# Two chunks of a GEGLU kernel turned later, and two of its weight columns moved to seven-product blocks

## The chip, the cores and the metric

One Trainium2 chip, one core of it. The metric is the device time of one execution in microseconds (us), as the median of three runs. A profile is one further execution, recorded by the hardware profiler; its span runs from its first to its last instruction. Engines are named as in the profile: PE is TensorE (matmuls; PEld its weight loads), DVE is VectorE, ACT is ScalarE, POOL is GpSimd, SP is SyncE, which issues most DMAs. Each engine works through its own queue in order.

## The reference

```python
def reference(x, dft_seq_re, dft_seq_im, dft_hid_re, dft_hid_im, w_gate, w_up, w_down):
    xn = layernorm(x)                          # x: 1 x 2048 x 448
    a = xn @ dft_hid_re.T                      # 448 x 448
    b = xn @ dft_hid_im.T
    s = dft_seq_re @ a - dft_seq_im @ b        # 2048 x 2048
    h = gelu(xn @ w_gate) * (xn @ w_up)        # 448 x 1792 each
    g = silu(h @ w_down)                       # 1792 x 448
    return x + s * g
```

## The kernel before

Tokens lie on 128 partitions in 16 tiles of 128, four tiles to a chunk; so there are four chunks (c = 0 to 3) of 512 tokens. The 1792 columns of the gate and the up matrix are cut into 14 columns f of 128. fp32 operands are split into a high part (rounded to the multiplication format, copied by ACT) and a low part (the rest, subtracted by DVE); a product of two split operands is three matmuls (high x high, high x low, low x high). The feature axis of 448 is four blocks of 128, the last with copies in it.

**Entry.** Rows of x are loaded into `xr`, normalised there (`stats`: bn_stats and bn_aggr on DVE, root on ACT, `newton` and `norm` on DVE), transposed by PE against an identity (`turn_mm`, L167, four small matmuls into one PSUM bank) and split into `xth` and `xtl` (`turn_split`, L172 on ACT, L178 on DVE). After a chunk's last tile `whole` copies the high parts to a DRAM tile `xw` with an SP DMA (L189), and adds the low parts to it with an accumulating DMA that POOL issues (L190). Pieces of that fp32 copy are read back later into temporaries (`t_load`, L674) and turned into sums.

**Direct columns.** Columns 0 and 1 of all four chunks are multiplied directly: `gateup` or `gu_mm` (L325) makes gate and up of one column and one chunk with 22 matmuls of 512 columns; `act` (L351 to L356) makes the gelu, the product and the split result `hs`. `down_one` (L376) makes one tile of the output of two columns: six matmuls of 448 columns into a PSUM bank, which is then copied (L385, ACT, the first pair of columns) or added (L387, DVE) into the sums `gacc`. The sums of chunks 0 and 1 stay in SBUF; those of chunks 2 and 3 are written to DRAM (`gsp`) after the first pair and read back in the second run.

**Two runs of blocks.** For columns 2 to 13, first for chunks 0 and 1 (run p = 0), then for chunks 2 and 3 (p = 1), `strassen` makes gate and up of one column for two chunks out of seven products with sums of the operands. A block has 41 matmuls of 512 columns where the operand sums `q` of the third and fourth feature blocks do not exist yet, and 39 where they do (L398, L410). Its results stand in PSUM banks 0 to 4: x1 in bank 0 (one product, read by ACT, L430, then a second product on top, read by the gelu, L456), x2 in bank 1, x3 and without `q` also x5 in bank 2, x4 in bank 3 (two products one after the other), x6 in bank 4. So x1 of the next block waits for the gelu L456 of this one, the next x3 for the DVE addition that reads x5 (L477) or x3, the next x4 for the one that reads x4 (L488). Between its products stand four places `dn` (the first behind x2, the last at the block's end), each for a `down_one` out of a list `dq` of pending output tiles (banks 5 to 7 in turn), and three places `prep` for preparing the next block's weights; the high part of these stands ahead of the gelu L456 in ACT's queue.

**Weights of a block.** `load_s` (L260, L261) loads a column's raw weights into the one raw buffer; `sums_s` forms their sums there (L276 to L280, five POOL operations); `split_s` makes high and low parts in three steps: plain (L289 ACT, L290 DVE), high (L293, L294 ACT), low (L297, L298 DVE). The next `load_s` stands behind L298, since the buffer is one.

**Order.** Nothing is reordered: the program records instructions in the order in which each engine's queue then holds them.

**Afterwards** come the hidden transform, the sequence transform (also by seven products) and the output.

Of the kernel before, what the change touches and what calls it, by code (L numbers as in the profile page):

```python
# [47 lines left out]
def fnet_geglu(ctx: ExitStack, tc: tile.TileContext, x, ca, ct, cp, et, wgu, wss, wd, out):  # L48
# [27 lines left out]
    a_x = [sb.tile([P, 4096], FR, name=f"xt{c}") for c in range(NC)]  # L76
    a_g = [sb.tile([P, 8 * D], F32, name=f"gacc{p}", tag=f"g{p}") for p in range(2)]
# [8 lines left out]
    a_d = [sb.tile([P, 1792], FR, name=f"wd{i}", tag=f"d{i}") for i in range(2)]  # L86
# [12 lines left out]
    xth = [part(a_x[c], 0, 4, 512) for c in range(NC)]  # L99
    xtl = [part(a_x[c], 2048, 4, 512) for c in range(NC)]  # L100

    a_u = [sb.tile([P, 2, 4, 512], F32, name=f"xr{p}", tag=f"u{p}") for p in range(2)]
    xr = [a_u[c // 2][:, c % 2] for c in range(NC)]
    gacc = [part(a_g[c // 2], c % 2 * 4 * D, 4, D) for c in range(NC)]
# [4 lines left out]
    turns = {"mm": 1, "tp": 0, "o": 0, "x": 0, "po": 0, "all": 0}  # L109

    def in_turn(kind, name):

        first, n = {"mm": (0, 4), "tp": (4, 2), "o": (6, 2), "x": (0, 5), "po": (5, 3), "all": (0, 8)}[kind]
        turns[kind] += 1
        return bank(first + turns[kind] % n, name)
# [47 lines left out]

    def turn_mm(c, k):
        pt = tp_tile(f"pt{c}_{k}").rearrange("p (b d) -> p b d", b=4)
        for b in range(4):
            nc.tensor.transpose(pt[:, b], xr[c][:, k, b * P : (b + 1) * P], ident)  # L167
        return c, k, pt

    def turn_split(*turned):  # L170
        for c, k, pt in turned:
            nc.scalar.activation(xth[c][:, :, k * P : (k + 1) * P], pt, AF.Copy)  # L172
        for c, k, pt in turned:
            if c < 2:
                nc.scalar.activation(xf[c][:, :, k * P : (k + 1) * P], pt[:, :2], AF.Copy)
# [3 lines left out]
        if k == 3:  # L179
            whole(c)  # L180

    xw = [dram.tile([P, 2048], F32, name=f"xw{c}") for c in range(NC)]

    def whole(c):
        n = 1024 if c < 2 else 0
        h, l = [a_x[c][:, 2048 * i + n : 2048 * (i + 1)].bitcast(F32) for i in range(2)]
        nc.sync.dma_start(xw[c][:, n:], h)  # L189
        nc.gpsimd.dma_start(xw[c][:, n:], l, accum_op=ALU.add)  # L190
# [3 lines left out]


    xf = [part(a_t, 1024 * (c + 1), 2, 512) for c in range(2)]

# [58 lines left out]
    def load_s(f):  # L256
# [3 lines left out]
        nc.sync.dma_start(r[:, 6:14], wss[f - 2][:, :8])  # L260
        nc.sync.dma_start(r[:, 0:17:16], wss[f - 2][:, 8:])  # L261
# [47 lines left out]
    def d_view(gi):  # L309
        return a_d[gi % 2].rearrange("p (a f d) -> p a f d", a=2, f=2)  # L310
# [1065 lines left out]
```

## Time and profile before

| | |
|---|---|
| median of three runs | 773.72 us (773.69 to 774.84) |
| span of the profiled execution | 770.7 us (no other time is recorded of it) |
| median less span | 3.0 us, taken as what lies around the span |
| PE busy in the span | 764.0 us of 770.7 |
| DVE, ACT, POOL busy | 638.5, 347.4, 124.9 us |
| granted TensorE clock, mean | 0.998 |

In rows of the profile, a line such as L376 is a line of the kernel before. A row of the timeline has its start, its duration, the engine, the line, what it writes and reads, and in brackets how long the engine had been idle and what released it. A row of the chain of waits has a start, a duration and what stood on the path that sets the end.

### The profile page before, as it was taken

Reading aid. Unit: us, or ns where it says so; the run is one execution under the profiler, and the core shown is the slowest. Engines: PE = TensorE matmul, PEld = TensorE weight load, DVE = VectorE, ACT = ScalarE, POOL = GpSimd, SP = SyncE. Lnnn points to the kernel's source line nnn. Section 1 sums busy time; section 2 is a strip of 40 time slices with the busy share of each in tenths; the row PEclk is TensorE's granted clock in tenths of the full one; section 3 lists DMA queues with packets and bytes.
Section 4 is the critical chain, followed back from the end, with each engine's and each line's share of the span. In section 5 each row is a group of like instructions: output and inputs, shape, how many; then the busy total and the mean of one; then the engine's idle time right before and its main releaser. Section 6 shows DMA issues by size and latency. Waiting matters only on the chain.

```text
span 770.7 us, 11500 instructions
## 1 busy us (share of the span) xinstructions
PE 764.0 (99%) x4052; PEld 688.3 (89%) x4052; DVE 638.5 (83%) x1093; ACT 347.4 (45%) x490; POOL 124.9 (16%) x162
## 2 busy tenths in 40 slices
PE   9999999999999999999999999999999999999997
PEld 8988888888888888888889999999999999999996
DVE  7978989898988988887885676889788796969797
ACT  3756444452533444344334855544444444444441
POOL 2003242332423323323200000000000000000000
PEclk9999999999999999999999999999999999999999
DMA  8479666566767746465652641879797969697894
GB/s 316 91 201 284 153 223 180 148 238 186 252 130 265 199 164 154 154 150 191 138 187 95 268 191 53 255 255 276 262 307 223 343 204 348 189 341 211 311 286 166
DMA packets 81322, 165.46 MB, mean 215 GB/s; under 512 B 8048, under 2 KB 62704, under 8 KB 79728
## 3 DMA queue, kind: packets, MB, share of 16 engines
q1 hardware_dynamic: 75648, 137.15, 51.7%
q0 software_dynamic: 5472, 27.46, 16.7%
q8 instruction: 32, 0.52, 0.3%
q14 instruction: 26, 0.21, 0.1%
q10 hardware_dynamic: 144, 0.11, 0.0%
HBM read 140.71 MB, written 53.35 MB: 252 GB/s over the span
## 4 chain that ended last, share of the span: by engine, by line
PE 95%; DVE 2%; DMA 1%; issue 0%; ACT 0%; SPq 0%; DVEq 0%
PE x L398 24%; PE p L1173 21%; PE po L376 18%; PE p L1176 10%; PE ab L989 9%; PE x L410 4%; PE gu L325 3%; PE py L1193 1%; PE py L1195 1%; PE py L1194 1%; DMA raw<-wgu 1%; PE gu L543 1%; PE pt L167 1%; DVE st L140 0%; DVE xr L158 0%
## 5 line engine op out<-in xcount | busy, mean ns | idle before, releaser
L376 PE MATMUL po<-wd,hs 128*128 128x448 f32 x672 | 152.7, 366 | 0.0
L376 PEld LDWEIGHTS po<-wd,hs 128*128 128x128 f32 x672 | 125.8, 188 | 14.2
L398 PE MATMUL x<-xt,w 128*128 128x512 f32 x450 | 119.4, 391 | 0.0
L398 PEld LDWEIGHTS x<-xt,w 128*128 128x128 f32 x450 | 84.4, 188 | 16.4 <-DVE tmp L444 0.4
L127 ACT ACTIVATE w<-raw 128x896 fp32r<-128x896 f32 (+1 forms) x59 | 53.7, 912 | 63.1 <-DVE raw L1079 35.4
L398 PE MATMUL x<-t,w 128*128 128x512 f32 x276 | 79.7, 391 | 0.0
L387 DVE TENSOR_TENSOR gacc<-gacc,po 128x448 f32<-128x448 f32 x96 | 58.5, 615 | 12.4 <-PE po L376 12.3
L989 PE MATMUL ab<-w,xt 128*128 128x448 f32 x256 | 68.1, 365 | 0.0
L398 PEld LDWEIGHTS x<-t,w 128*128 128x128 f32 x276 | 51.8, 188 | 9.3
L1218 POOL DMA_DIRECT2D cc<-x x14 | 12.4, 882 | 289.3 <-DVE raw L1078 107.8
L475 ACT ACTIVATE hs<-tmp 128x512 fp32r<-128x512 f32 x24 | 15.2, 634 | 97.4 <-DVE tmp L473 97.4
L1173 PE MATMUL p<-xt,w 128*128 128x448 f32 x168 | 54.3, 374 | 0.0
L276 POOL TENSOR_TENSOR raw<-raw 128x256 f32<-128x256 f32 x23 | 18.5, 806 | 211.9 <-DMA raw<-wss 177.4
L989 PEld LDWEIGHTS ab<-w,xt 128*128 128x128 f32 x256 | 48.1, 188 | 3.8
L127 ACT ACTIVATE w<-f 128x896 fp32r<-128x896 f32 (+1 forms) x34 | 30.2, 889 | 42.1 <-DVE f L1079 21.1
L128 DVE TENSOR_TENSOR w<-raw,w 128x896 fp32r<-128x896 f32 (+1 forms) x40 | 41.8, 1046 | 3.3 <-ACT w L127 2.7
L1078 DVE TENSOR_TENSOR raw<-raw 128x128 f32<-128x128 f32 x69 | 19.8, 287 | 21.2 <-DMA raw<-sums 21.1
L293 ACT ACTIVATE w<-raw 128x768 fp32r<-128x768 f32 x24 | 20.3, 846 | 36.7 <-POOL raw L280 36.7
L1173 PE MATMUL p<-ts_u,ts_tmp 128*128 128x448 f32 x112 | 36.3, 374 | 0.0
L1173 PE MATMUL p<-ts_g,w 128*128 128x448 f32 x112 | 36.3, 374 | 0.0
L410 PE MATMUL x<-xt,w 128*128 128x512 f32 x116 | 35.9, 390 | 0.0
L1173 PE MATMUL p<-hs,w 128*128 128x448 f32 x112 | 35.6, 374 | 0.0
(267 smaller groups left out, 1842.8 us busy)
## 6 DMA issues: line engine op xcount, KB each, us to landing
sums<-ca SPq DMA_DIRECT2D x16, 896.0 KB, 8.7
sums<-ca POOLq DMA_DIRECT2D x16, 896.0 KB, 8.6
raw<-ct SPq DMA_DIRECT2D x69, 192.0 KB, 4.4
raw<-wss SPq DMA_DIRECT2D x24, 512.0 KB, 3.9
ts_u<-td SPq DMA_DIRECT2D x24, 448.0 KB, 6.3
ts_g<-td SPq DMA_DIRECT2D x24, 448.0 KB, 6.5
raw<-sums SPq DMA_DIRECT2D x69, 128.0 KB, 4.4
f<-ct SPq DMA_DIRECT2D x39, 192.0 KB, 3.8
```

What stands on the lines that cost most here:

```text
L127: nc.scalar.activation(h, src, AF.Copy)
L128: nc.vector.tensor_sub(l, src, h)
L293: nc.scalar.activation(h[:, :n], src[:, :n], AF.Copy)
L325: nc.tensor.matmul(ps[:, cols], a, xt[:, k, cols], start=n == 0, stop=n == len(mm) - 1)
L376: nc.tensor.matmul(po[:, :D], hs[:, a, kk * P : (kk + 1) * P], wdn[:, b, i], start=n == 0, stop=n == 5,)
L387: nc.vector.tensor_add(ga, ga, po[:, :D])
L398: nc.tensor.matmul(ps, a[i], b[j], start=first and n == 0, stop=n == 2, skip_group_check=True)
L410: nc.tensor.matmul(ps, a[0], x_, start=False, stop=True, skip_group_check=True)
L989: nc.tensor.matmul(p[:, :D], a, b, start=n == 0, stop=n == len(mm) - 1)
L1078: nc.vector.tensor_add(s2, cr1, s1)
L1173: nc.tensor.matmul(ps[q][:, :D], h, v, start=u % UN == 0, stop=False, skip_group_check=True)
L1176: nc.tensor.matmul(ps[q][:, :HD], l, v[:, :HD], start=False, stop=u % UN == NS - 1, skip_group_check=True,)
```

## The change

Chunks 2 and 3 are not turned at the entry. Their rows wait in a tile `rows` (and `tmp(1)`), their statistics are made by ACT (`row_stats`: two activations that sum along a row; one of the first four tiles is done by bn_stats on DVE), and POOL normalises them (`row_norm`). They are turned in blocks of the first run: chunk 2 in columns 4 and 5, chunk 3 in column 6, behind the `down_one` of a `dn` place. Columns 0 and 1 of chunks 2 and 3 become two more seven-product blocks at the start of the second run, so the second run has columns 0 to 13. The sums of chunks 2 and 3 are now built up in the second run alone and the tiles `gsp` go. The fp32 forms of chunks 0 and 1 that the operand sums need are kept in SBUF (`xf`, full width) in the space of the later `xt2` and `xt3`; so `whole` is for chunks 2 and 3 only, the `q` sums of the first run are made by POOL (four subtractions) ahead of the first block, and `q` is in use from column 4 on (before: from column 5). The first block's weight sums go from DVE to POOL. The order of loading `load_s(2)` and `load_s(3)`, and which columns get which places, moves with it. Of the 4,054 matmuls in the program 4,042 are left; the 12 that go are 512 columns wide.

```diff
+        def row_stats(i):
+            n = slice(i, i + 1)
+            nc.scalar.activation(waste, row(i)[:, :D], AF.Identity, scale=-1.0 / D, accum_out=neg[:, n])
+            nc.scalar.activation(waste, row(i)[:, :D], AF.Square, bias=neg[:, n], accum_out=ssq[:, n])
+        def row_root(c):
+            n = slice(4 * c - 8, 4 * c - 4)
+            nc.scalar.activation(dev[:, n], ssq[:, n], AF.Sqrt, bias=epst, scale=1.0 / D)
+        def row_norm(i):
+            n = slice(i, i + 1)
+            nc.gpsimd.tensor_scalar(
+                row(i), row(i), neg[:, n], inv[:, n], op0=ALU.add, op1=ALU.mult
+            )
...
-        wdn, d_low = prep_d(GROUPS[0], draw)
-        one(0)
+        nc.vector.bn_stats(st, rows[:, 3, :D])
...
+        wdn, d_low = prep_d(draw)
+        row_root(2)
         d_low()
...
-        turn_split(t2, t3)
-        one(1)
         m0, h0, l0 = act(0, 0, pgs[0])
         m1, h1, l1 = act(1, 0, pgs[1])
+        for c, k, pt in c1:
+            nc.scalar.activation(xf[c][:, :, k * P : (k + 1) * P], pt, AF.Copy)
+        draw = load_d(GROUPS[1])
+        load_s(2)
         m0()
         h0()
         m1()
         h1()
-        one(2)
...
+        row_newton(2)
+        qa, qe, qb, qf = [xf[n][:, k] for k in (3, 2) for n in range(2)]
+        both = a_f[0][:, 2048:2560]
+        for r in (slice(0, 64), slice(64, P)):
+            nc.sync.dma_start(both[r], qf[:64])
+        nc.gpsimd.tensor_sub(qa, qe, qa)
+        nc.gpsimd.tensor_sub(qe, both, qe)
+        nc.gpsimd.tensor_sub(qf[:64], qf[:64], qa[:64])
+        nc.gpsimd.tensor_sub(qb, qb, qf)
+        sums_s(nc.gpsimd)
+        q0 = {1: qa, 2: qf, 3: qe, 4: qb}
+        t0 = combine(*[xf[n][:, k] for n in range(2) for k in range(2)])
...
-        turn_split(turn_mm(2, 0))
         h0()
-        between = [lambda k=k: turn_split(turn_mm(2, k)) for k in (1, 2, 3)]
...
+        down(0, 0, wdn, [t_split0(2), l1, t_split0(3), t_split0(4)])
+        w_of = {(0, 2): parts_of(slots[0])}
+        down(0, 1, wdn, split_s(slots[0]))
+        load_s(3)
+        nwdn, low_d = prep_d(draw)
...
-        dq = [(0, 3, wdn, kk) for kk in range(4)]
+        dq = []
...
-        blocks = [(p, f) for p in range(2) for f in range(2, NF)]
+        blocks = [(p, f) for p in range(2) for f in range(2 - 2 * p, NF)]
...
+                if f < 4:
...
+                    dn = [nop] * 4
...
+                if f == 2:
+                    for i in range(4):
+                        row_norm(i)
+                elif f in (4, 5):
+                    for i in range(2):
+                        k = 2 * (f - 4) + i
+                        dn[1 + 2 * i] = then(dn[1 + 2 * i], lambda k=k: turn_split(turn_mm(2, k)))
+                        prep[1 + i].append(lambda k=k: row_stats(4 + k))
+                elif f == 6:
+                    for i in range(4):
+                        row_norm(4 + i)
+                        dn[i] = then(dn[i], lambda k=i: turn_split(turn_mm(3, k)))
...
             late = strassen(f, p, w_of[p, f], q, late, dn, prep)
+            if p == 0:
+                if f == 5:
+                    whole(2)
+                    row_root(3)
+                    row_newton(3)
+                elif f == 6:
+                    whole(3)
+                elif f == 7:
+                    t_load(0, 1, 0, 1)
```

More of the change, by code (lines that the diff above doesn't have):

```diff
@@ L72, in fnet_geglu @@
     dram = ctx.enter_context(tc.tile_pool(name="dram", bufs=1, space=bass.MemoryType.DRAM))
[L76 to L77 removed]
+    a_x = [sb.tile([P, 4096], FR, name=f"xt{c}", tag=f"x{c}") for c in range(2)]
+    a_f = [sb.tile([P, 4096], F32, name=f"xf{c}", tag=f"x{2 + c}") for c in range(2)]
+    a_g = sb.tile([P, 8 * D], F32, name="gacc0", tag="g0")
+    rows = sb.tile([P, 7, DX], F32, name="rows", tag="g1")
     a_ws = sb.tile([P, 7680], FR, name="w")
@@ L85, in fnet_geglu @@
     ]
-    a_d = [sb.tile([P, 1792], FR, name=f"wd{i}", tag=f"d{i}") for i in range(2)]
+    a_d = [sb.tile([P, 1792], FR, name=f"wd{i}", tag=f"d{1 - i}") for i in range(2)]
     a_r = sb.tile([P, 7 * D], F32, name="raw")
@@ L601, in fnet_geglu @@
         one(1)
+        row_stats(1)
+        row_stats(2)
         root()
@@ L775, in sum_step @@
                     nc.gpsimd.dma_start(a, b, accum_op=ALU.add)
-        gsp = [dram.tile([P, 4 * D], F32, name=f"gsp{c}") for c in range(2)]
         sp = dram.tile([P, 4096], F32, name="sp")
```

224 lines of the change are left out of this document (95 added, 129 removed).

## The prediction

> **What bounds the kernel now.** I read the page's header and busy times first, then PE's own waits, then the chain that ended last from 17 to 136 us, then the timeline of the weights' preparation. Of the page:
>
> ```profile
> span 770.7 us, 11500 instructions
> ...
> PE 764.0 (99%) x4052; PEld 688.3 (89%) x4052; DVE 638.5 (83%) x1093; ACT 347.4 (45%) x490; POOL 124.9 (16%) x162
> ```
>
> PE's waits over the whole span, by length:
>
> ```profile
> PE warm L524 <- DVE hs L514: 1.5, 1, 1.5
> PE gu L543 <- ACT xt L172: 0.3, 1, 0.3
> ```
>
> PE is never held once it has started, except for 0.3 us at the entry (L543). So matmuls that go are gained in full, and every new wait of PE is lost in full: nothing behind it has slack to give the time back. The chain of waits (start, duration, what):
>
> ```profile
> 28.95 5.02 PE gu L325 x22
> 33.97 0.44 PE pt L167 x4
> ...
> 72.19 4.08 PE x L398 x18
> ...
> 76.73 1.21 PE po L376 x6
> ...
> 83.93 4.10 PE x L398 x18
> ```
>
> A 512-column matmul takes 4.08/18 = 0.227 us, an output tile 1.21, a turned tile 0.44. Column 2's block lasts 83.93 - 72.19 = 11.74 us with two output tiles in it; without them 41 matmuls are 9.3 us.
>
> **A: the matmuls.** Direct columns 0 and 1 of chunks 2 and 3 go: 4 x 22 = 88. Two blocks come, 41 + 39; column 4 of the first run and column 2 of the second fall from 41 to 39. 80 - 4 - 88 = -12, by 0.227: **-2.7 us**, all on the path. Output tiles and turned tiles are as many as before. The DMAs that go (gsp both ways, half of the xw copies) and the DVE work that goes (statistics, norms) give nothing: PE waited for none of them.
>
> **B: the entry.** These rows of the timeline price it:
>
> ```profile
> 24.32 0.61 DVE L140 BATCH_NORM_STATS2 st<-xr 128x6 f32<-128x448 f32 x1
> ...
> 24.55 1.19 ACT L172 ACTIVATE xt<-pt 128x512 fp32r<-128x512 f32 x2 [0.82 <-PE pt L167]
> ...
> 24.87 4.08 PE L543 MATMUL gu<-xt,w 128*128 128x256 f32 x32
> ...
> 63.02 0.68 DVE L209 TENSOR_TENSOR tmp<-tmp 128x512 f32<-128x512 f32 x1
> ...
> 66.00 0.55 ACT L385 ACTIVATE gacc<-po 128x448 f32<-128x448 f32 x1 [0.67 <-PE po L376]
> ```
>
> The six `row_stats` activations of the entry I put at nothing: some 6 x 0.55 = 3.3 us on an engine that is busy 45% of the span; without that cover the norm behind the next root is late by up to 1 us. But `row_root(2)` now stands ahead of the two copies at 24.55 and waits for the statistics of row tile 3 on DVE, some 1.2 us after 24.32, so the copies end near 26.9, not 25.74. PE needs them ten half-width matmuls (4.08/32 = 0.13 each) after the tiles turned until 25.1, at 26.4: +0.5. From there along the queues, in steps of 0.55 to 0.7 as in these rows: table load (1.28, a row under D) and two gelus, 29.3; the first product on DVE, the second, 30.6; five small operations of `row_newton`, 1.0; the four of `combine`, 0.7 each; then only, near 34.7, the low part of block (0,0), whose temporary gelu (0,1) waits for. Before, neither `row_newton` nor `combine` stood there. On: gelu 35.3, product 36.0, copy 36.7, t1's high part 37.2, gelu (1,1) 37.8, product 39.2, copy 39.8, and only then ACT empties the first output bank, 40.3. PE ends gate/up (1,1) at 28.95 + 0.5 + 5.0 = 34.5 and four output tiles later, at 39.4, wants that bank: +0.9. The low part of (1,1), behind a `t_split0`, is 0.7 late in the same way. **B = +2.1**, between 0.5 (the copies alone) and 3 (POOL's four subtractions late as well).
>
> **C: columns 2, 3, 4.** A block's weights are a cycle through one raw buffer: load, POOL sums, high part, low part, next load.
>
> ```profile
> 79.67 0.33 SPq L260 DMA_DIRECT2D raw<-wss  x1
> ...
> 85.51 0.75 POOL L276 TENSOR_TENSOR raw<-raw 128x256 f32<-128x256 f32 x1 [9.98 <-DMA raw<-wss]
> ...
> 89.35 0.73 POOL L280 TENSOR_TENSOR raw<-raw 128x256 f32<-128x256 f32 x1
> ...
> 90.11 0.85 ACT L293 ACTIVATE w<-raw 128x768 fp32r<-128x768 f32 x1 [3.35 <-POOL raw L280]
> ...
> 90.99 0.96 DVE L297 TENSOR_TENSOR w<-raw,w 128x768 fp32r<-128x768 f32 x1 [0.65 <-ACT w L293]
> ...
> 91.69 0.58 ACT L456 ACTIVATE tmp<-x 128x512 f32<-128x512 f32 x1
> ...
> 91.98 0.69 DVE L298 TENSOR_TENSOR w<-raw,w 64x512 fp32r<-64x512 f32 x1
> ...
> 92.70 0.33 SPq L260 DMA_DIRECT2D raw<-wss  x1
> ...
> 94.71 0.68 DVE L477 TENSOR_TENSOR tmp<-tmp,x 128x512 f32<-128x512 f32 x1
> ...
> 106.82 0.33 SPq L260 DMA_DIRECT2D raw<-wss  x1
> ...
> 111.38 0.74 POOL L276 TENSOR_TENSOR raw<-raw 128x256 f32<-128x256 f32 x1 [7.19 <-DVE tmp L488]
> ...
> 114.64 0.74 POOL L280 TENSOR_TENSOR raw<-raw 128x256 f32<-128x256 f32 x1
> ```
>
> From load to load it took 13.0 and 14.1 us. Its parts: 4.6 to 5.8 from load to sums, 4.0 to 4.6 of sums, 2.6 from there to the next load: 11.2 to 13.0 at best. Blocks of 11.7 us and more could live with that, since weights were ready early: column 4's at 91.95 (row 90.99) for a block that began near 95.7 (83.93 + 11.8). Now columns 2 and 3 hold no output tile: 9.3 us each, shorter than any cycle. And there is no lead: the first block's sums stand on POOL behind four subtractions that wait for a DMA, and its low part ends 1.8 us after the block began, which is when the next load starts. What this does, with B for a block's start: load lands at +6.4; DVE waits for it ahead of its reading of x3 (L290 is first in its queue), so x5 is 1.7 late; sums done +10.5, high part +11.3, the gelu behind it on ACT +12.2, and x1 of column 3 waits for that gelu. Its x3 waits for DVE, which after the low weights (+12.2) has the five operations of the rows 91.98 to 94.71, 3.4 us, so +15.6. That is 4.9 later than 9.3 + 1.4 would be. The next cycle, 11.2 to 13.0 against 9.3, adds 1.9 to 3.7 less some of what column 4's longer block regains. **C = +7**, between 3.5 (cycles of 11, and DVE through earlier) and 10 (14-us cycles).
>
> **D: column 6.** Chunk 3's first tile is turned behind x2 and one output tile, 0.227 x 11 + 1.21 = 3.7 us into the block. Its norm stands on POOL behind the accumulating DMA of `whole(2)`, and that waits for SP's copy to land, which waits for ACT's copy of the tile turned at the very end of column 5. In this kernel such a pair looked like this:
>
> ```profile
> 25.77 0.33 SPq L189 DMA_DIRECT2D xw<-xt  x1
> ...
> 29.91 0.87 POOL L190 DMA_DIRECT2D xw<-xt  x1 [6.26 <-DVE tmp L354]
> ...
> 30.21 1.28 ACT L145 ACT_TABLE_LOAD   x1
> ...
> 55.44 0.33 SPq L189 DMA_DIRECT2D xw<-xt  x1
> ...
> 60.80 0.89 POOL L190 DMA_DIRECT2D xw<-xt  x1 [14.19 <-DVE w L290]
> ```
>
> Whatever the brackets name, both POOL rows follow the SP rows by 4.1 and 5.4 us. Nothing but this copy hung on it then. Now: ACT 0.7 + landing 5 + POOL 0.9 = 6.6, then norms. No row has a norm on POOL; bounds are the rows
>
> ```profile
> 8.80 1.85 POOL L235 TENSOR_TENSOR w<-raw,w 128x768 fp32r<-128x768 f32 x1 [7.48 <-DVE w L230]
> ...
> L277 POOL TENSOR_TENSOR raw<-raw 128x256 f32<-128x256 f32 x23 | 24.1, 1048 | 0.0
> ```
>
> 1.85 x 512/768 = 1.2 below, 2 x 1.05 = 2.1 above; I take 1.2, since this one reads one tile, not two. PE gets the tile at 7.8 instead of 3.7: +4.1. Worse follows: all four norms stand ahead of `sums_s` for column 7, which end at 6.6 + 4.8 + 4.2 = 15.6, and ACT's queue holds its high part ahead of the gelu (with a table load, 1.28, since the root came between) and of the second turned tile's copy: 15.6 + 0.85 + 0.4 + 1.28 + 0.6 + 0.6 = 19.3. DVE then needs 0.7 for the tile's low part and 3.7 for five more until it has emptied the bank that the fourth turned tile wants: 23.7. Unhindered the block ends at 39 x 0.227 + 4 x 1.21 + 4 x 0.44 = 15.5; so it ends at 24.1. **D = +8**, between 3.0 (the first norm alone, with a 4.1 us landing) and 12 (norms of 2.1).
>
> [...]
>
> **E: behind it.** Column 8's sums stand on POOL behind `whole(3)` in the same way: copy 0.7, landing 5, three POOL issues 2.6, sums 4.2, high part and gelu 2: some 14.5 us after column 7's start, against a block of 13.75. **E = +1.5**, between 0 and 5, since column 6's backlog on DVE makes the copy later.
>
> **The sum.** -2.7 + 2.1 + 7 + 8 + 1.5 = +15.9 on the span of 770.7: 786.6, and with the 3.0 us that the median (773.7) has beyond the span, **789.6 us**.
>
> **Rivals.** *Shorter waits* (R1): the same places, each at its lower bound: -2.7 + 0.5 + 3.5 + 3.0 + 0 = +4.3, **778.0**. For it: DMA traffic is lighter without half the copies, so landings may come at 4.1 to 4.6 us from issue; against it: the load of row 79.67 took 5.8. *Faster* (R2): the preparation stays hidden, only A counts: **771.0**. It needs SP's copy to land within 1.1 us in column 6 (3.7 - 0.7 - 0.9 - 1.0) and a weight cycle under 9.3; from there on the sign turns. The shortest seen are 4.1 and 13.0, so little speaks for it beyond that queues may run otherwise than I read them. *Slower still by the clock* (R3): PE would stand 4 us at one place for the first time. Its longest wait before is 1.5 us, at the start, and the granted clock was 0.998 on the mean, so no row shows what 4 us do. If such a wait halved the matmul rate for as long as it lasted, 4.1 us of work would take twice that, 2 us lost, at column 6 twice and perhaps at column 8: +4.5, **794**. [...] *That the change does not do what it says* is out: the twelve matmuls are gone from the built program.
>
> **Numbers.** Forecast, 783 to 797: 0.60. R1 and what lies near it, 775.5 to 783: 0.19. R3 or norms of 2.1, 794 to 802: 0.12. R2: 0.07. Between 772.2 and 775.3: 0.02. The range from 777 to 799 leaves out R2, the edge of R1 and the top of R3. About 0.2% (1.5 us) is what a measurement of this kernel can tell from no change: faster by more 0.07, within it 0.02, slower 0.91.
>
> **What would show it.** Right: PE waits by name, for the gelu and for DVE's reading of x5 in columns 3 and 4 (near 55 to 75 us), for POOL's norm in column 6 with 4 us in one piece, POOL's `xw` issue directly ahead of it; 12 matmuls fewer, and after column 8 PE without gaps to the end. Wrong: POOL's four norms done before column 6 begins (D falls to 0); block starts in columns 2 to 4 at 9.3 and 9.3 us (C falls); a time under 775; or a granted clock well under 0.99 (then R3, and the sum is right for the wrong reason).

## The result and the profile after

| | before | after |
|---|---|---|
| median, us | 774.28 (773.69 to 776.85, 4 runs) | 811.63 (810.54 to 812.78, 4 runs) |
| span of the profiled execution, us | 770.7 | 808.8 |
| granted clock, mean | 0.998 | 0.987 |

The changed kernel is slower: ratio 1.0479, 95% interval 1.0458 to 1.0500; 38.1 us on the span, where +15.9 was forecast. The page after (its header, the busy times, the chain of waits by engine):

```profile
span 808.8 us, 11517 instructions
...
PE 774.4 (96%) x4040; PEld 688.2 (85%) x4040; DVE 640.6 (79%) x1080; ACT 360.1 (45%) x525; POOL 144.8 (18%) x187
...
PE 69%; DVE 10%; DMA 6%; POOL 5%; ACT 5%; issue 3%; SPq 0%; DVEq 0%; POOLq 0%; ACTq 0%
```

PE is no longer the whole path. Its own waits after (engine, line, what it waited for: us in total, times, longest):

```profile
PE pt L176 <- POOL rows L628: 8.2, 1, 8.2
PE po L380 <- DVE hs L357: 4.0, 3, 2.1
PE x L402 <- DVE tmp L481: 3.2, 2, 2.0
PE x L402 <- DVE tmp L453: 2.9, 2, 1.8
PE x L402 <- ACT tmp L460: 2.3, 2, 1.9
...
PE pt L176 <- DVE xt L187: 1.4, 1, 1.4
PE po L380 <- ACT gacc L389: 1.4, 1, 1.4
```

Every forecast wait is there by name: the gelu (L460), DVE's reading of x5 (L481), POOL's norm (L628) in one piece, the entry's output tiles (L357, L389). To compare places I take each column's length from the first matmul of its x1 to that of the next column's, less its matmuls at full rate (read from the traces where the granted clock is 1.00: 0.227 us for 512 columns, 0.202 for 448, 0.1275 for 256, 0.099 for 224, 0.11 for a transpose). What is left is its loss, in us, for the two kernels and for the experiments below that the account rests on:

| place | before | after | e_noq | e_latesums | f_root | f_entry | f_all | i_hybrid |
|---|---|---|---|---|---|---|---|---|
| entry | 4.6 | 13.1 | 8.7 | 12.0 | 12.0 | 5.6 | 5.3 | 6.6 |
| columns 2 to 4 | 0.4 | 9.1 | 9.5 | 5.5 | 9.2 | 9.1 | 8.9 | 5.8 |
| column 5 | 0.1 | 0.7 | 0.6 | 0.6 | 0.6 | 0.6 | 0.6 | 0.7 |
| column 6 | 0.1 | 11.6 | 11.4 | 11.7 | 4.1 | 12.2 | 2.7 | 2.6 |
| columns 7, 8 | 0.1 | 5.3 | 5.2 | 0.5 | 7.6 | 5.9 | 8.4 | 2.3 |
| columns 9 to 13 | 0.4 | 3.3 | 4.1 | 0.4 | 2.9 | 3.1 | 4.1 | 0.6 |
| column 0, second run | – | 3.5 | 3.5 | 1.2 | 3.0 | 3.5 | 3.5 | 1.2 |
| all behind it, transforms too | 16.2 | 16.1 | 16.1 | 33.7 | 16.2 | 16.4 | 16.3 | 17.9 |
| span | 770.7 | 808.8 | 805.3 | 811.6 | 801.7 | 802.6 | 796.0 | 783.8 |

After less before: 8.5 + 8.7 + 0.6 + 11.5 + 5.2 + 2.9 + 3.5 - 0.1 = 40.8, and with the twelve matmuls (2.7) that went, the 38.1. The second run loses nothing behind its column 0. The entry has some play: in e_norms, e_warm, f_root and e_latesums, whose edits lie behind it, it lost 12.0 to 12.8 instead of 13.1, so a difference of 1 us there is no effect of an edit.

Where the chain of waits runs in column 3, and in column 8 (start, duration, what):

```profile
63.33 0.34 SPq L260
...
63.72 6.94 DMA raw<-wss
...
70.83 0.73 POOL raw L276
71.56 1.28 POOL raw L277
...
74.54 0.86 ACT w L293
...
151.64 0.34 SPq L260
...
152.03 9.32 DMA raw<-wss
```

It is the cycle through the one raw buffer, as forecast; but the load, for which the forecast had 4.6 to 5.8 us to the first sum, takes 6.9 and 9.3 itself.

### The profile page after: what moved, and what is told of

It is laid out like the page before. It is cut to its first block, busy times and chain, and to the rows that moved or that the text cites. A ratio compares the mean times of both kernels' runs of the same rounds, so it can differ in the third digit from the quotient of the medians.

```text
span 808.8 us, 11517 instructions
## 1 busy us (share of the span) xinstructions
PE 774.4 (96%) x4040; PEld 688.2 (85%) x4040; DVE 640.6 (79%) x1080; ACT 360.1 (45%) x525; POOL 144.8 (18%) x187
## 4 chain that ended last, share of the span: by engine, by line
PE 69%; DVE 10%; DMA 6%; POOL 5%; ACT 5%; issue 3%; SPq 0%; DVEq 0%; POOLq 0%; ACTq 0%
PE p L1195 20%; PE x L402 12%; PE po L380 10%; PE p L1198 10%; PE ab L1011 9%; DMA raw<-wss 6%; PE x L414 2%; PE py L1215 1%; PE py L1217 1%; PE py L1216 1%; POOL raw L277 1%; DVE w L297 1%; DVE w L298 1%; ACT w L293 1%; POOL raw L280 1%
## 5 line engine op out<-in xcount | busy, mean ns | idle before, releaser
L380 PE MATMUL po<-wd,hs 128*128 128x448 f32 x672 | 154.7, 369 | 5.9 <-DVE hs L357 4.0
L402 PE MATMUL x<-xt,w 128*128 128x512 f32 x486 | 131.9, 398 | 6.7 <-DVE tmp L453 2.9
L402 PEld LDWEIGHTS x<-xt,w 128*128 128x128 f32 x486 | 90.6, 189 | 28.8 <-ACT tmp L460 4.4
L402 PE MATMUL x<-t,w 128*128 128x512 f32 x298 | 89.9, 402 | 4.3 <-DVE tmp L481 3.2
L402 PEld LDWEIGHTS x<-t,w 128*128 128x128 f32 x298 | 56.6, 192 | 16.3 <-DVE tmp L481 4.0
L276 POOL TENSOR_TENSOR raw<-raw 128x256 f32<-128x256 f32 x26 | 22.5, 867 | 220.1 <-DMA raw<-wss 162.3
L479 ACT ACTIVATE hs<-tmp 128x512 fp32r<-128x512 f32 x26 | 16.4, 632 | 94.2 <-DVE tmp L477 94.2
L293 ACT ACTIVATE w<-raw 128x768 fp32r<-128x768 f32 x26 | 22.0, 844 | 55.1 <-POOL raw L280 55.1
L290 DVE TENSOR_TENSOR w<-raw,w 128x640 fp32r<-128x640 f32 x26 | 25.5, 981 | 17.0 <-ACT w L289 16.9
L414 PE MATMUL x<-xt,w 128*128 128x512 f32 x122 | 38.3, 396 | 0.2 <-DVE w L298 0.2
L297 DVE TENSOR_TENSOR w<-raw,w 128x768 fp32r<-128x768 f32 x26 | 24.8, 955 | 15.4 <-ACT w L293 15.3
## 6 DMA issues: line engine op xcount, KB each, us to landing
sums<-ca POOLq DMA_DIRECT2D x16, 896.0 KB, 10.2
```

Of the source, the lines that this page charges most:

```text
L290: nc.vector.tensor_sub(l[:, n:], src[:, n:WL], h[:, n:WL])
L293: nc.scalar.activation(h[:, :n], src[:, :n], AF.Copy)
L297: nc.vector.tensor_sub(l[:, :n], src[:, :n], h[:, :n])
L380: nc.tensor.matmul(po[:, :D], hs[:, a, kk * P : (kk + 1) * P], wdn[:, b, i], start=n == 0, stop=n == 5,)
L402: nc.tensor.matmul(ps, a[i], b[j], start=first and n == 0, stop=n == 2, skip_group_check=True)
L414: nc.tensor.matmul(ps, a[0], x_, start=False, stop=True, skip_group_check=True)
```

## The experiments

All are edits of the changed kernel, except where another is named. Four accounts stood against each other first: O, each queue order has its own cost at its place; L, one lost lead of the weight loads makes everything behind it late; P, DVE and POOL slow each other; K, the granted clock that drops in PE's waits (0.50 from 115 to 125 us, at the longest) is the cost.

**e_low: the entry's low parts first.**

```diff
         h1()
+        l0()
+        l1()
         row_newton(2)
...
-        l0()
-        l1()
```

> Edit: of the changed kernel (811.6 us) only the entry's DVE queue is reordered: the low parts of blocks (0,0) and (1,0) stand ahead of row_newton and the four combine operations, not behind them. Account O (order in the queues): the third gelu (0,1) comes some 4 us earlier (33 instead of 37.2 us), output tiles start without the waits of 2.1 and 0.8 us for hs, the entry's loss of 8.5 us falls by about 3, and nothing of it is given back: 808 to 809. Account L (the entry's loss is set by the weights of column 2 being late, the rest follows from the lost lead): output tiles come earlier but the first block's weights do not, since POOL's sums still end at 42; under 2 us gained, 810 to 812. Account P (POOL's subtractions slow DVE whatever its order): the two low parts, now at 30 us, still take over 2.5 us for the pair, and the gain is 1 to 2.

811.38 us (ratio to the kernel before 1.0475, interval 1.0451 to 1.0498; from here on the interval alone stands in brackets): nothing gained. The entry lost 12.2 instead of 13.1, within its play, and columns 2 to 13 gave it back; the load for column 3 was issued at 52.1 instead of 52.7. The order that I had named for B, `combine` ahead of the low parts, is not what costs by itself.

**e_lead: the weights of column 2 first.**

```diff
+        sums_s(nc.gpsimd)
         nc.gpsimd.tensor_sub(qa, qe, qa)
...
-        sums_s(nc.gpsimd)
...
+        high()
+        down(0, 0, wdn, [l1, lambda: (low(), load_s(3)), t_split0(2), t_split0(3)])
-        down(0, 1, wdn, split_s(slots[0]))
-        load_s(3)
+        down(0, 1, wdn, [t_split0(4)])
```

> Edit: as the one before, and besides POOL makes the weight sums of column 2 ahead of its four q subtractions, the split of these weights stands in the first group of output tiles instead of the second, so the load for column 3 is issued some 11 us earlier (near 41 instead of 52.7 us), and the norms of chunk 2 stand on POOL behind the sums for column 3. Account L (lost lead: one late load runs on through the single raw buffer to all later columns): loss in the entry 8.5 -> 3, in columns 2 to 5 9.4 -> 3, and in columns 6 to 13 and the first of the second run some 5 of 23 us go as well: 793 to 797. Account O (each place has a cost of its own): only entry and columns 2 to 5 gain, columns 6 and later keep their 23 us: 799 to 802. If the cycle of 13 us against blocks of 9.3 us is the whole of C, columns 2 to 5 keep 6 or more: 803.

807.82 us (1.0397 to 1.0441). A miss: the load came at 47.6, not 41, and the entry lost 13.9. Only columns 2 and 3 gained, 4.2 together (the load for column 3 now started 5.4 us before column 2 began), and column 10 took 2.4 of it back. What held the entry is in DVE's queue: `combine`, ahead of the next product, now met POOL's subtractions, and its last two operations took 1.67 and 1.63 us.

**e_norms: norms ahead of the accumulating DMA.**

```diff
-                        row_norm(4 + i)
...
-                    whole(2)
                     row_root(3)
                     row_newton(3)
+                    for i in range(4):
+                        row_norm(4 + i)
+                    whole(2)
```

> Edit: of the changed kernel only POOL's order ahead of column 6 is changed: the four norms of chunk 3 stand ahead of the accumulating DMA of chunk 2, not behind it. The sums for column 7 still stand behind that DMA. Account O: PE's wait of 8.2 us for the norm in column 6 goes, but the sums for column 7 still come some 11 us into the block, so column 6's loss falls from 11.6 to about 4 and the time to 803 to 805. Account L (weights are late anyway, so the wait only changes its name): column 6 keeps 8 us or more, now under the gelu or DVE, 808 to 811. [...]

807.98 us (1.0409 to 1.0450). Column 6 still lost 9.2, instead of 11.6. The timeline of column 6, first in the changed kernel, then in this one:

```profile
108.58 0.93 PE L402 MATMUL x<-xt,w 128*128 128x512 f32 x3
...
113.90 0.58 ACT L181 ACTIVATE xt<-pt 128x512 fp32r<-128x512 f32 x1
114.50 1.28 ACT L616 ACT_TABLE_LOAD   x1
114.50 0.34 SPq L193 DMA_DIRECT2D xw<-xt  x1
...
119.84 0.92 POOL L194 DMA_DIRECT2D xw<-xt  x1 [17.59 <-DVE gacc L391]
120.52 2.53 POOL L628 TENSOR_SCALAR rows<-rows,neg,inv 128x512 f32<-128x512 f32 x3
121.63 1.11 PE L176 MATMUL pt<-ident,rows 128*128 128x128 f32 x4 [8.22 <-POOL rows L628]
```

```profile
112.70 0.58 ACT L181 ACTIVATE xt<-pt 128x512 fp32r<-128x512 f32 x1
113.30 1.28 ACT L616 ACT_TABLE_LOAD   x1
...
114.92 0.17 DVE L620 TENSOR_SCALAR ssq<-ssq 128x4 f32<-128x4 f32 x1 [0.92 <-ACT dev L616]
...
115.95 2.32 POOL L628 TENSOR_SCALAR rows<-rows,neg,inv 128x512 f32<-128x512 f32 x2 [14.89 <-DVE inv L624]
...
117.06 1.11 PE L176 MATMUL pt<-ident,rows 128*128 128x128 f32 x4 [4.84 <-POOL rows L628]
```

With the DMA out of the way the norms still wait for the root (L616), which stands on ACT behind the copy of the last turned tile of chunk 2, and that copy comes 5.3 us after the block's first matmul (108.58) in the changed kernel. Neither O nor L had this wait.

**e_warm: PE kept busy in its long wait.**

```diff
+        if (c, k) == (3, 0):
+            for _ in range(24):
+                nc.tensor.matmul(pt.rearrange("p b d -> p (b d)"), xth[0][:, 0, :P], xth[0][:, 0], start=True, stop=True)
         for b in range(4):
```

> Edit: of the changed kernel, 24 extra matmuls of 512 columns (5.5 us at full rate, results overwritten) stand on PE in column 6 directly ahead of the first turned tile of chunk 3, inside its wait of 8.2 us. They leave 3 us of idle time there. Account K (the halved clock after long waits costs much of the difference): the granted clock stays at 1 from 115 to 125 us, what follows the wait runs at full rate, and the time falls by 2 to 3 us, to 808.5 to 809.5. Accounts O and L (the clock is a by-product while DVE, ACT and POOL set the end of column 6): within 1 us of 811.6.

811.94 us (1.0455 to 1.0494). Busy time and granted clock (the column behind POOL's) from 115 to 126 us, in the changed kernel and in this one:

```profile
115.00:122.00 7.00, 0.37 (x2) 0.37 (x3) 3.35 (x10) 2.19 (x4) 2.15 (x3) 0.50 0.83 235
122.00:126.00 4.00, 4.00 (x14) 3.29 (x13) 2.44 (x2) 1.43 (x2) 3.96 (x7) 0.60 0.96 193
```

```profile
115.00:122.00 7.00, 4.98 (x25) 3.90 (x24) 3.16 (x9) 1.86 (x5) 2.54 (x4) 1.00 0.82 227
122.00:126.00 4.00, 4.00 (x19) 3.36 (x18) 3.27 (x2) 1.39 (x2) 3.92 (x7) 1.00 1.03 211
```

The clock stays at 1.00 as meant and the time does not move. PE ran 19 matmuls instead of 14 in the four microseconds behind the wait and then waited more, since ACT, DVE and POOL set the end of the column. K is refuted at its longest wait. Three more stretches of 3.4 us each stood at half clock in the changed kernel, in the entry (0.50 from 46.7 us), column 3 (0.51 from 67.2) and column 8 (0.50 from 152.5). At half rate they cost at most 1.7 us each, an estimate from their length; no run takes them away alone.

**e_noq: without POOL's four subtractions.**

```diff
-        nc.gpsimd.tensor_sub(qa, qe, qa)
-        nc.gpsimd.tensor_sub(qe, both, qe)
-        nc.gpsimd.tensor_sub(qf[:64], qf[:64], qa[:64])
-        nc.gpsimd.tensor_sub(qb, qb, qf)
```

> Edit: the changed kernel without POOL's four subtractions for q in the entry (they are left out, so the operand sums of the third and fourth feature blocks are not formed; all else is as it was). Account P (DVE and POOL slow each other when both work on SBUF, and this makes most of the entry's loss): combine's last operation takes 0.7 instead of 1.66 us and the two low parts behind it 1.3 instead of 3.4, POOL's sums for column 2 end at 36 instead of 42, the entry's loss of 8.5 us over the kernel before falls to 4 or 5: 806 to 808. Account O (the order on DVE and ACT alone makes the loss): the third gelu still waits for the same operations, under 1.5 us gained: 810 to 811.6.

808.51 us (1.0427 to 1.0462). The entry's loss fell from 13.1 to 8.7. DVE and POOL in the entry of the changed kernel (timeline: start, duration, what, and in brackets the idle time and who ended it):

```profile
33.05 0.69 DVE L211 TENSOR_TENSOR xf<-xf,xf 128x512 f32<-128x512 f32 x1
33.23 1.65 POOL L692 TENSOR_TENSOR xf<-xf,xf 128x512 f32<-128x512 f32 x1 [1.76 <-DMA xf<-xf]
33.78 1.66 DVE L212 TENSOR_TENSOR xf<-xf,xf 128x512 f32<-128x512 f32 x1
34.84 1.71 POOL L693 TENSOR_TENSOR xf<-xf,xf 64x512 f32<-64x512 f32 x1
35.36 3.43 DVE L357 TENSOR_TENSOR hs<-tmp,hs 128x512 fp32r<-128x512 f32 x2
36.63 1.61 POOL L694 TENSOR_TENSOR xf<-xf,xf 128x512 f32<-128x512 f32 x1
...
37.16 0.87 PE L380 MATMUL po<-wd,hs 128*128 128x448 f32 x3 [2.06 <-DVE hs L357]
...
38.20 1.18 POOL L276 TENSOR_TENSOR raw<-raw 128x256 f32<-128x256 f32 x1
38.72 0.68 DVE L355 TENSOR_TENSOR tmp<-tmp,gu 128x512 f32<-128x512 f32 x1
```

and the same stretch without the subtractions:

```profile
33.86 0.69 DVE L212 TENSOR_TENSOR xf<-xf,xf 128x512 f32<-128x512 f32 x1
34.14 1.00 POOL L276 TENSOR_TENSOR raw<-raw 128x256 f32<-128x256 f32 x1 [22.55 <-DMA raw<-wss]
34.47 2.38 DVE L357 TENSOR_TENSOR hs<-tmp,hs 128x512 fp32r<-128x512 f32 x2
```

L212 takes 0.69 alone and 1.66 beside POOL; the pair L357 takes 3.43 beside the subtractions (and 2.38 here, where POOL's sums run beside it). Where both have such operations waiting, each engine does one in some 1.7 us (1.61 to 1.71 on POOL), as if they took turns; what makes them do so is not shown. L355, which reads one operand from PSUM, takes 0.68 beside POOL's L276.

**f_root, f_entry, f_all: root, norms and copies moved together; entry reordered; both.** f_root, where `late_norms` is `row_root(3)`, `row_newton(3)` and the four `row_norm`:

```diff
+                    if f == 5:
+                        prep[2].append(late_norms)
...
-                        row_norm(4 + i)
...
+                if f in (6, 7):
+                    prep[0].append(lambda c=f - 4: whole(c))
...
-                if f == 5:
-                    whole(2)
-                    row_root(3)
-                    row_newton(3)
-                elif f == 6:
-                    whole(3)
```

> Edit: of the changed kernel only what surrounds column 6: the root, the Newton step and the four norms of chunk 3 follow its last row statistics inside column 5 (they stood behind the last turned tile of chunk 2), and the two copies of chunks 2 and 3 to DRAM are issued inside columns 6 and 7, behind POOL's sums. Account O: with the norms done before column 6 begins and no accumulating DMA ahead of the sums, PE's wait for the norm is 0, column 6's loss 11.6 -> 2 to 3, columns 7 and 8 together 5.2 -> 2 to 3: 798 to 801. Account L (weights come late whatever stands there): column 6 keeps 5 us or more, under the gelu or DVE: 803 to 806.

f_entry (its core; `q_sums` is POOL's four subtractions and `row_newton(2)`):

```diff
         m0()
+        t0 = combine(*[xf[n][:, k] for n in range(2) for k in range(2)])
+        plain, high, low = split_s(slots[0])
+        plain()
...
+        down(0, 0, wdn, [lambda: (low(), load_s(3)), t_split0(2), t_split0(3), t_split0(1)])
...
-        dq = []
+        dq = [(0, 1, wdn, kk) for kk in range(4)]
...
+                        dn = [send, send, send, then(send, low_d)]
+                    if f == 2:
+                        prep[2].append(q_sums)
```

> Edit: of the changed kernel only the entry and columns 2 and 3. On DVE the low parts and the product of block (0,1) stand ahead of combine, the Newton step goes into column 2; POOL makes the weight sums of column 2 first, its q subtractions go into column 2, the q splits all into column 3; the weights of column 2 are split during the first four output tiles, so the load for column 3 is issued near 40 instead of 52.7; the other four output tiles go from the entry into column 3. Expected by O and P together: entry's loss of 8.5 -> 2 to 4, columns 2 to 5 9.4 -> 2 to 4: 798 to 801. By L, the lead that the earlier loads give stays and columns 6 to 10 gain 3 or more besides: 794 to 797. If the weight cycle of 13 us against blocks of 9.3 is the whole of C, the entry gains and column 3 and 4 keep 5: 803.

> Edit: the two before together. If the places add: 811.6 less some 11 for each, 788 to 791. If the lost lead joins them, columns 10 and 0 of the second run (6 us) shrink as well: 783 to 787. Even with no wait left, twelve matmuls fewer give 771, so the kernel before (774) is not expected to be beaten by this order alone.

Measured: f_root 804.71 us (1.0372 to 1.0406), f_entry 804.11 (1.0367 to 1.0408), f_all 796.20 (1.0267 to 1.0305). On the spans the two edits bring 7.1 and 6.2, and together 12.8: the places add, as O has it. But each brings little more than half of what O expected, and both times lie where the other accounts had them (f_root's in the range of L, f_entry's near the 803 expected for the weight cycle). f_root takes column 6 from 11.6 to 4.1, and column 7 takes 2.8 back. f_entry takes the entry from 13.1 to 5.6; columns 2 to 4 still lose 9.1. In f_all column 7 alone loses 6.1. There the load issued at 116.2, for column 8, was not summed before 133:

```profile
113.39 2.06 POOL L780 DMA_DIRECT2D sums<-ca  x2
...
116.23 0.34 SPq L260 DMA_DIRECT2D raw<-wss  x1
...
132.95 0.72 POOL L276 TENSOR_TENSOR raw<-raw 128x256 f32<-128x256 f32 x1 [17.51 <-DMA raw<-wss]
```

The window from 115 to 130 us of the same run (the DMA engines' share is the last number but one):

```profile
115.00:130.00 15.00, 15.00 (x75) 12.79 (x74) 10.96 (x18) 4.30 (x7) 0.44 (x1) 1.00 1.02 222
```

The DMA engines are full, at 1.02. Beside the load run two accumulating copies `sums<-ca` of 896 KB each, which prepare the sequence transform and are issued every third column; plain copies of the same size stand between them. Neither my forecast nor O or L had them. Call this account W.

**e_latesums: the copies kept out of the first run.**

```diff
-            sum_step(n)
+            if n > 12:
+                sum_step(2 * n - 26)
+                sum_step(2 * n - 25)
```

> Edit: the changed kernel with the copies that prepare the sequence sums (from ca into sums, 896 KB each, plain and accumulating) kept out of columns 2 to 13 and of column 0 of the second run; they are done twice as densely in the thirteen blocks from column 1 of the second run on. Nothing else moves. Account W (the weight load for a block lands late where it meets these copies, and without a lead PE pays for it): the loads of columns 7 to 10 land after 4 to 6 instead of 9 to 10 us, the losses of columns 7, 8 and 10 (7.8 us together) fall below 3, and the second run, whose loads have a lead, pays under 2 us: 805 to 808. Account L (the lateness comes from the first columns alone): these losses stay, 810 to 812. Column 0 of the second run (3.4 us) goes if its wait for the temporaries is this traffic, and stays if it is the order of its operand steps.

816.13 us (1.0522 to 1.0565), since all that stands behind its column 0, with the copies twice as dense, lost 17.6 more. But the first matmul of column 0 now began at 227.65 instead of 240.14 us (first the changed kernel, then this one):

```profile
240.14 0.96 PE L402 MATMUL x<-xt,w 128*128 128x512 f32 x3
```

```profile
227.65 0.86 PE L402 MATMUL x<-xt,w 128*128 128x512 f32 x3
```

Columns 7 to 13 lost 0.8 instead of 8.6, columns 2 to 4 5.5 instead of 9.1, column 0 of the second run 1.2 instead of 3.5. Together that is 13.7 us from column 2 to there, the cost of the copies in the changed kernel. The run does not separate two ways in which they can act: they stand on the DMA engines beside the loads (a share of 1.02 in the window of f_all), and POOL issues the accumulating ones ahead of its sums, which took it 2.04 us for two in column 7 of the changed kernel (L783, at 143.88). The load of column 4's weights, in the chain of waits:

```profile
62.52 0.33 SPq L260
...
62.95 3.73 DMA raw<-wss
```

3.73 us instead of 6.94. That the second run would pay under 2 us was wrong. The expectations that follow count columns from a later matmul of the block, so single losses in them differ from the table's by up to 2 us (14.6 us for the 13.7 here, 7.8 for column 7's 6.1 in f_all).

**g_spread, g_best: copies one by one.** g_spread (an edit of f_all):

```diff
-                halves = halves[:1] if j == 0 else []
-            elif d == 2 and j == 0:
+                halves = halves[:1]
+            elif d == 2:
```

> Edit: f_all (796.2 us) with the two accumulating copies of each sequence sum put into two columns instead of both into one (7, 10, 13 and so on). Account W: column 7, where the weight load took over 10 us beside both of them, loses 2 to 4 instead of 7.8 us, columns 10 and 13 together 1 to 2 instead of 3.8: 788 to 791. If the copy of chunk 2 alone fills the queues, column 7 keeps 6 or more: 794 to 796.

g_best is g_spread with the entry's weights ahead of its low parts, two deferred tiles in column 2, the last operand step of the second run in column 1, and this for columns 2 and 3:

```diff
+                    high, low = prep[1].pop(0), prep[2][:2]
+                    del prep[2][:2]
+                    dn[2] = then(dn[2], high)
+                    dn[3] = then(*low, dn[3])
```

> Edit: g_spread, and besides: on ACT and DVE the weights of column 2 and its second operand sum stand ahead of the low parts that only later output tiles need; the Newton step stands ahead of POOL's q subtractions; two of the four deferred output tiles go into column 2; in columns 2 and 3 the splitting of the next weights stands two places later, behind the gelu; the last operand step of the second run moves from its column 0 to column 1 (two more matmuls, +0.45). Expected from the losses of f_all: entry and column 2 from 11.0 to 5, column 4 from 1.9 to 1, column 0 of the second run from 3.4 to 1 or 2: 779 to 784. If DVE, 90% busy in these columns, sets the pace instead, 786 to 790.

Two misses: g_spread 800.25 us (1.0326 to 1.0370; its profiled span, 796.2, is that of f_all) and g_best 801.36 (1.0327 to 1.0365). In g_spread column 7 fell from 6.1 to 0.2, but column 8 lost 6.9, as DVE waited 7.0 us for a temporary read back from the copy of chunk 3, which f_all had put into column 7, and column 9 lost 4.4 behind a load of 12.2 us: the meeting moved on by a column. In g_best entry and column 2 fell from 9.5 in g_spread to 6.5, half of what was expected, but with the splitting two places later columns 3 and 4 had to wait for their weights (PE waited 1.8 us for L297 and 3.6 for L298; the two columns lost 8.5 instead of 5.0).

**h_pieces, h_final, i_hybrid: the copies between two loads.** h_pieces is an edit of the changed kernel; `pieces` is the list of the 32 copies of 896 KB, each issued by POOL:

```diff
-            sum_step(n)
+            prep[0].extend(pieces.pop(0) for _ in range(1 + (12 <= n < 18)))
```

> Edit: of the changed kernel only the copies into the sequence sums are moved in time: one of the 32 pieces of 896 KB per block (two in blocks 12 to 17, in the second run), each issued by POOL behind its weight sums, that is after this block's load has landed and some 5 us ahead of the next one's issue. Account W (in the kernel with these copies kept out, the first run was 14.6 us shorter): the losses of columns 3 and 4 (6.5 us) fall to 3, those of columns 7 to 13 (9.9 us) to under 2, the second run pays under 2 us: 799 to 803. If a piece in any place collides with the next load: 808 to 812.

> Edit: f_all (796.2 us) with these pieces, and in the entry on ACT and DVE the weights of column 2 and its second operand sum ahead of the low parts that only later output tiles need, the Newton step ahead of POOL's q subtractions, two of the four deferred output tiles in column 2 and two in column 3. Losses expected: entry and column 2 5.5, columns 3 to 6 4, columns 7 to 13 1, column 0 of the second run 2, where the changed kernel has 41: 776 to 780. Over 786 would say that a cause is missing from the list (entry's order, weight cycle, column 6's order, DVE against POOL, the large copies).

i_hybrid differs from h_final in

```diff
-            prep[0].extend(pieces.pop(0) for _ in range(1 + (12 <= n < 18)))
+            if n < 12:
+                prep[0].append(pieces[n])
+            else:
+                sum_step(n - 3)
+                if n == len(blocks) - 1:
+                    sum_step(n - 2)
```

> Edit: h_final (789.9 us) with the pieces of the sequence sums laid out otherwise in the second run: in the first run one piece of 896 KB per block behind POOL's sums, as in h_final; in the second run the old steps and places of the changed kernel, begun three blocks later. In h_final the blocks of the second run with two pieces each lost some 10 us, in the changed kernel its columns 1 to 13 lost none. Account W: these losses fall to 2 or 3, the first run keeps its loss: 782 to 785. If the old places cost in the second run as they did in the first, 788 to 792.

Measured: h_pieces 806.35 us (1.0413 to 1.0451), h_final 789.90 (1.0203 to 1.0237), i_hybrid 784.59 (1.0099 to 1.0166). In h_pieces, which missed its range by 3, the second run began 11.0 us earlier, and what follows gave 6.8 of it back, 5.3 in its columns 0 and 4 to 7, in or just behind the blocks with two pieces. In i_hybrid, which does not double them, the second run loses nothing from column 1 to 12. h_final missed its range by 10, half of which went with this last edit; i_hybrid met its own. It stays 11 us slower than the kernel before, so no version here beats it; its granted clock was 0.999, so the clock has hardly a part in these 11.

**b_late: the kernel before, with its loads later.**

```diff
-        if f in GROUPS[1] and p == 0:
-            preps[2]()
-            dn[1]()
-        else:
-            dn[1]()
-            preps[2]()
+        dn[1]()
...
         dn[3]()
+        preps[2]()
```

> Edit: the kernel before (774), with the low part of the next weights, and with it the next load, put at the end of each block, some 4 us later; no other work moves. Account L and W (the kernel before pays nothing for slow loads because its loads start 4 to 9 us ahead of need): PE then waits in the columns whose loads land after 7 to 8 us (columns 7, 10, 13 and around), 2 to 4 us each: 782 to 792. If the lead is not what protects it: 773 to 776.

842.96 us (1.0835 to 1.0925), far more than expected. (In column 2 of each run an operand difference is then formed behind its split, so two operand sums hold other values.) Nearly every column lost 1.9 us or more, up to 5.7: PE waited for L298, the low part itself, 39.3 us in 20 places. So the kernel before has no 4 us to spare in this cycle. It is evidence that the early splitting protects it, but it does not isolate the slow loads, since the low parts come late too.

## Why the prediction was wrong

The direction was right, and so were most places and the names of the waits. The sizes of all terms but the first were too small, and one cause was missing. Forecast and measured (loss after less before):

| term | forecast | measured |
|---|---|---|
| A, twelve matmuls | -2.7 | -2.7 |
| B, entry | +2.1 (0.5 to 3) | +8.5 |
| C, columns 2, 3, 4 | +7 (3.5 to 10) | +8.7 |
| D, column 6 | +8 (3 to 12) | +11.5 |
| E, column 8 | +1.5 (0 to 5) | +5.2 (columns 7, 8) |
| not in the forecast: columns 5, 9 to 13, column 0 of the second run | 0 | +7.0 |

Two steps of the prediction failed. It mis-sized B (6.4 of the 22.2 us that the sum lacked), and it put the `sums<-ca` copies at nothing, without naming them: 13.7 us, which lie in C, in E and in the places that were not in the forecast. C and D stayed within their bounds, D by their width.

- **B** is the step that failed first. I walked the queues "in steps of 0.55 to 0.7 as in these rows", rows from a stretch where POOL was idle, and gave POOL's four subtractions a place in the upper bound only as being "late as well". They do not only come late, they slow DVE: 1.66 for 0.69. Taking them out lowered the entry's loss by 4.4 (3.3 against the lowest entry with them); the order I had blamed, alone, by 0.9, within the entry's play, and the time by nothing. That POOL's sums then come earlier too is not what helped by itself: e_lead began them at 32.3 instead of 38.2, and its entry lost no less. A part of the 4.4 may be the clock, which stood at 0.50 for 3.4 us in the entry of the changed kernel; its mean over the profiled execution was 0.987 there and 0.993 in e_noq, and no run separates the two. The other half of the entry's 8.5 went in f_entry, which moved several operations at once, so which of them cost it stays open.
- **C** was the right mechanism. Its size came from landings of "4.6 to 5.8 from load to sums"; the loads of columns 4 and 5 took 7.0 and 7.2 us. The kernel before had shown it: its load issued at 92.70, between the two that I read, was summed only at 100.15, 7.5 us later. With the copies out the two loads took 3.8 and 4.2, and columns 2 to 4 lost 5.1 over the kernel before; 3.7 belong to the copies.
- **D**'s chain was right in length and wrong in its start. From the copy of the last turned tile to the norms I had 0.7 + 5 + 0.9 = 6.6 us; the rows have 113.90 to 120.52, 6.6. The norms themselves were shorter than my 1.2 us each: from 120.52 to the end of the fourth it took 3.25. But I let that copy stand at the block's start, and it came 5.3 us in, behind DVE and ACT work that was late itself. I also left the root, its table load and the Newton step out of the way to the norms: e_norms shows that they alone keep the norm 3.3 us behind that copy.
- **E** had the wrong cause. In e_latesums `whole(3)` still stands ahead of the sums, and columns 7 and 8 together lose 0.5. It was the copies, on the DMA engines or in POOL's queue.
- **"After column 8 PE without gaps to the end"** was wrong by 6.4 us, 2.9 in columns 9 to 13 (mostly column 10) and 3.5 in column 0 of the second run; 2.9 and 2.3 of it go with the copies.
- **"DMA traffic is lighter without half the copies, so landings may come at 4.1 to 4.6 us"** (R1) looked at the wrong transfers: the `sums<-ca` copies stayed, 896 KB each, and the kernel before has slow loads too (7.2 and 8.1 us in columns 6 and 9), at no cost.
- **R3** came half true: its condition held, its price did not. That a long wait halves the rate was a supposition then, which no row of the kernel before shows. In the changed kernel the granted clock stood at 0.50 for 10.2 us at column 6, from 115.0 to 125.2 us, around a wait of 8.2; keeping it at 1.00 brought nothing there (e_warm, 811.94 us).

So of the 38.1 us, by experiments: 13.7 the copies (columns 2 to 4 3.7, 7 to 13 7.8, column 0 of the second run 2.3); 8.5 the entry, about half of it with POOL's subtractions; 11.5 column 6, of which 7.5 went when root, norms and copies to DRAM were moved; less 2.7 for the matmuls. What columns 2 to 4 lose without the copies, 5.1, is put down to the weight cycle in short columns by the chain of waits, and some 2 are unassigned (1.2 of it in column 0 of the second run).

What is argued and not shown is why the second run bears the same copies at the same density without loss, as the kernel before does; b_late points to the early splitting, but no run takes that lead away alone. The traces fit it. In the kernel before, from column 4 on, a column's load is issued 0.9 to 4.1 us before the block ahead of it begins, and in the changed kernel's second run, from column 2 on, 1.5 to 3.8 us before. In its first run it is between 1.0 us before and 1.1 behind (2.5 before, once). The load issued at 351.44, 2.8 us before that block, took 8.2 us and cost nothing. The one at 151.64, 0.1 us behind its start, took 9.5 and stands in the chain of waits. In f_root a load issued 2.9 us before took 10.2, and column 7 lost 5.1, so this much lead does not cover every load.

## What to carry to other kernels

When a change moves matmuls away, list what they were covering: here 20 us of direct columns had given DVE, ACT, POOL and the loads time to get ahead, and several places that were free with that lead had a price without it. Do not take an operation's duration from a stretch in which its neighbour was idle: look for a row of the same form beside POOL at work (here 1.66 us instead of 0.69). And for each load that becomes critical list all transfers that can be in flight with it, not only those that the change touches (here 6.94 us instead of 3.73 for column 4's weights).

## What the runs showed of the hardware

- A DVE operation of 128x512 with both operands in SBUF took up to 1.66 us instead of 0.69 (L212) beside POOL's subtractions in SBUF, and these took 1.61 to 1.71 (L692 to L694); with one operand in PSUM it took 0.68 beside POOL's L276 (L355). Small ones paid as well: a Newton step of four elements (L623) took 1.15 us beside the first subtraction (L691) and 0.16 without it (e_noq).
- The granted clock halved where PE had no wait of more than 2.0 us: stretches of 3.4 us in which PE was busy 1.28 and 1.41 us, with longest waits of 1.4 and 2.0, were each followed by 3.4 us at 0.50 and 0.51. The windows of the changed kernel (PE's busy time is the second number, the clock the third from the end):

```profile
43.30:46.70 3.40, 1.28 (x5) 0.86 (x5) 1.85 (x3) 3.40 (x8) 2.21 (x3) 1.00 0.00 0
46.70:50.10 3.40, 3.39 (x9) 3.05 (x10) 2.01 (x3) 2.21 (x4) 0.00 (x0) 0.50 0.01 2
63.80:67.20 3.40, 1.41 (x7) 0.95 (x6) 3.30 (x6) 1.18 (x3) 0.00 (x0) 0.99 0.91 180
67.20:70.60 3.40, 3.40 (x10) 2.40 (x9) 2.00 (x4) 1.40 (x4) 0.00 (x0) 0.51 0.79 249
```

- A load of 640 KB took 3.73 us with the `sums<-ca` copies kept out (e_latesums, at 62.95 in the chain of waits); in the changed kernel, beside copies of 896 KB issued ahead of it, it took 6.94 (at 63.72), 9.32 (152.03) and 10.28 (181.58). In f_all, where the DMA engines' share was 1.02, one took 16.7 us from its issue to the first sum (116.23 to 132.95).
